# A second-layer tile cut in two around a first-layer tile, late results in other PSUM banks, and a load issued ahead of a transposition

## The chip, the core and the metric

The kernel runs on one core of a Trainium2 chip. The core has a matrix engine (TensorE; PE in the profile, with PEld for its weight loads), a vector engine (VectorE, DVE), an activation engine (ScalarE, ACT), a general engine (GpSimd, POOL) and a queue engine (SyncE, SP) that issues nearly all DMA transfers here. The engines run side by side, each through its own list of instructions in order, and wait for each other by semaphores. Matrix results go to PSUM, eight banks of 512 float32 per partition; everything else on the chip lies in SBUF.

The metric is the device time of one execution in microseconds (us). Lower is better.

## The reference

A retention layer (attention with a decay in place of the softmax) on 8 batches and 8 heads of 576 positions, and behind it a feed-forward block on the 4608 rows that come out:

```python
def _attn_ref(q, k, v):                       # q, k, v: (8, 8, 576, 64)
    scores = scale * np.matmul(q, k.transpose(0, 1, 3, 2))
    gamma = 1.0 - 2.0 ** (-5.0 - np.arange(H, dtype=np.float32))
    rel = pos[:, None] - pos[None, :]
    Dmat = np.where(rel >= 0, gamma[:, None, None] ** rel[None, :, :], 0.0)
    return np.matmul(scores * Dmat[None], v)
...
def _moe_ref(x, w_in, w_out, g_ln):           # x: (4608, 512)
    h = x @ w_in                              # (512, 1024): the first layer
    e = np.exp(h - np.max(h, axis=-1, keepdims=True))
    solu = h * (e / (np.sum(e, axis=-1, keepdims=True) + 1e-09))
    mu = np.mean(solu, axis=-1, keepdims=True)
    var = np.mean((solu - mu) ** 2, axis=-1, keepdims=True)
    ln = (solu - mu) / np.sqrt(var + 1e-06) * g_ln
    return ln @ w_out                         # (1024, 512): the second layer
```

## The kernel before

**Tiles.** The work is cut twice into 36 pieces. A retention step i (0 to 35) takes four heads over a window of 256 positions; a window is two steps, and the last window of every four batches holds the 64 left-over positions of each of them, loaded in four DMAs of 32 partitions per tensor. A feed-forward tile t (0 to 35) takes 128 of the 4608 rows. Tile t needs both steps of its window, so the two kinds of work run interleaved, the tiles some steps behind.

**Names.** One step or tile is a chain of operations, and the code, the diff and the text below call each by its kind and number:

- ldq, ldk, ldv: the loads of a step, on SP's queue (`load`). sq, sk, cv: scaling and casts of them, mostly on POOL.
- T: transposition of q and k on TensorE (`qk_tp`), Te: its evacuation to SBUF on ScalarE. S: scores, 16 matmuls into the bank pair s; mask: VectorE applies the decay. K, st, sm, sc: the running state. I and V: the two parts of the retention result in xy; xe: its evacuation on ScalarE into xT, the first layer's input.
- M1: the first layer of a tile, eight matmuls into h, two banks with one buffer for all tiles (`mm1`). ex: the exponential, on ScalarE. so: h times the exponential, on VectorE, into solu, which has six buffers. When ex and so have read h, the next M1 may write it.
- lx: transposition of solu by a DMA on SP's queue (`ln_dma`). Only the last tile is transposed on TensorE instead (L35, evacuated by Le35).
- va, or bnA and bnB: the variance, on ScalarE or in two halves on VectorE. fx, fin, rs: the scale per row, from the variance of both tiles of a window.
- M2: the second layer of a tile, eight matmuls into one bank (`mm2`). oe: ScalarE scales the result by rs and evacuates it to o_sb, which has three buffers (`o_ev`). out: its store (`store`). The last tile's second layer is done in two halves of columns, M2_35 and M3, with the evacuations oe35 and oz.
- cnt, cs, ci: a test on the row sums at the end, by which a branch picks a general path; it is not taken here.

**Order.** Nothing is scheduled at run time. `ORDER` lists, for each engine, all operations in the order in which the engine runs them; `plan` states each operation's dependencies and the buffers that it takes and frees; `order_ops` merges the five lists into one program order. So a moved word in `ORDER` is a moved instruction on that engine and nothing else, as long as the dependencies allow it.

**Banks of the second layer.** `home(t)` says in which bank M2 of tile t accumulates. Early tiles use s, which they share with the scores: S of a step waits until oe of the M2 before it has read s. Late tiles use o2, two banks taken in turn, which only open when the tile tl of the step transpositions is closed (`bank`), that is when the last Te has run. `OT` is the first tile in o2:

```python
def home(t):
    return "h" if t == NT - 1 else "o2" if t >= OT else "xy" if late(t) and t % 2 else "s"
```

L35 takes a turn in o2 as well.

Of the kernel before, what the change touches and what calls it, by code (L numbers as in the profile page):

```python
# [1081 lines left out]
```

## Time and profile before

| | us |
|---|---|
| median of three runs | 210.21 |
| the three runs | 209.46, 210.21, 211.24 |
| the profiled execution, whole | 208.5 |
| its span, first to last instruction | 206.7 |
| M1 matmuls (L713), 288 of them: busy, mean of one | 68.4, 0.380 |
| M2 matmuls (L786), 296 of them: busy, mean of one | 67.6, 0.373 |
| exponential (L721), mean of one | 1.022 |
| solu (L736 or, with an accumulated sum, L731), mean of one | 1.224 or 1.221 |
| evacuation of xy (L702), mean of one | 0.736 |
| half of a variance on VectorE (L742), mean of one | 0.681 |

The table's durations of matmuls overlap: they are pipelined, so the distance between the starts of two groups says what one costs, not the sum of its durations. A row of the timeline gives the start, the duration, the engine, the source line, the operation with the tile written and the tiles read, how many instructions it merges and, in brackets, how long the engine was idle before it and what released it. All times in the rows count from the start of the span.

### The profile page before, as it was taken

The page shows a single profiled execution, that of the slowest core. Times are in us where ns is not written, and L with a number is a line of the kernel's source. Part 1 is how long each engine was busy: PE and PEld are TensorE (multiplying, and loading weights), DVE is VectorE, ACT ScalarE, POOL GpSimd, SP SyncE. Part 2 cuts the span into 40 slices and gives each one's busy share as a digit, 9 for nine tenths or more (in the row PEclk, how much of TensorE's full clock was granted, in tenths as well). Part 3 has the DMA queues.
Part 4 walks back from the last instruction along what each step waited for, and adds up shares of the span by engine and source line. Part 5 has one row for each costly group of instructions (what it writes and reads, how often), then busy time and mean ns, then how long its engine had stood idle before and what let it go on. Part 6 is the DMA issues. An engine that isn't in the chain of part 4 may idle for free. (4 is left out here: it accounts for less than half of the span.)

```text
span 206.7 us, 8546 instructions
## 1 busy us (share of the span) xinstructions
PE 195.5 (95%) x3576; PEld 108.3 (52%) x3576; DVE 151.4 (73%) x269; ACT 140.7 (68%) x250; POOL 140.2 (68%) x235
## 2 busy tenths in 40 slices
PE   7996989999999999999999999999999999999981
PEld 2442654665665555555555555565555555544450
DVE  6575779995988878688897857896878685725850
ACT  2375798897776667667866687696868756576451
POOL 7434758999997797987678888789795853121110
PEclk9999999999999999999999999999999999999999
DMA  6999999999977869999999999999989557998734
GB/s 175 344 358 331 327 318 292 294 263 290 244 220 222 248 197 306 228 284 219 265 291 174 221 296 239 217 255 227 326 132 280 124 117 201 165 236 212 115 149 103
DMA packets 91112, 49.12 MB, mean 238 GB/s; under 512 B 29624, under 2 KB 84928, under 8 KB 91072
## 3 DMA queue, kind: packets, MB, share of 16 engines
q1 hardware_dynamic: 90832, 48.38, 96.3%
q8 instruction: 28, 0.46, 1.0%
q10 hardware_dynamic: 240, 0.18, 0.4%
q14 instruction: 12, 0.10, 0.2%
HBM read 32.56 MB, written 9.44 MB: 203 GB/s over the span
## 5 line engine op out<-in xcount | busy, mean ns | idle before, releaser
L713 PE MATMUL h_ps<-w_in,xT 128*128 128x512 f16 x288 | 68.4, 380 | 0.2 <-DVE solu L736 0.2
L786 PE MATMUL o_ps<-w2c,ev 128*128 128x512 f16 (+1 forms) x296 | 67.6, 373 | 0.0
L721 ACT ACTIVATE e_sb<-h_ps 128x1024 f32<-128x1024 f32 x36 | 36.8, 1022 | 23.7 <-PE h_ps L713 17.3
L656 DVE TENSOR_TENSOR ret<-s_ps,masks 128x1024 f16<-128x1024 f32 x36 | 43.9, 1219 | 11.2 <-PE s_ps L620 10.7
L786 PEld LDWEIGHTS <-ev 128*128 128x128 f16 x296 | 28.9, 98 | 33.0
L713 PEld LDWEIGHTS <-xT 128*128 128x128 f16 x288 | 25.4, 98 | 29.3 <-ACT xT L702 0.7
L477 POOL TENSOR_TENSOR q<-rawq,small 128x512 f16<-128x512 f32 x34 | 35.3, 1042 | 7.3 <-DMA rawq<-in_q_dram 6.6
L736 DVE TENSOR_TENSOR solu<-h_ps,e_sb 128x1024 f16<-128x1024 f32 x22 | 26.9, 1224 | 18.0 <-ACT e_sb L721 17.8
L477 POOL TENSOR_TENSOR k<-rawk,small 128x512 f16<-128x512 f32 x34 | 35.3, 1042 | 6.3 <-DMA rawk<-in_k_dram 5.9
L795 ACT ACTIVATE o_sb<-o_ps,rs 128x512 f32<-128x512 f32 (+1 forms) x37 | 25.0, 675 | 19.3 <-PE o_ps L786 7.7
L742 DVE BATCH_NORM_STATS2 bs<-solu 128x6 f32<-128x512 f16 x44 | 29.8, 681 | 0.1
L702 ACT CAST xT<-xy 128x512 f16<-128x512 f32 x36 | 26.5, 736 | 2.8 <-PE xy L580 2.7
L697 POOL CAST sbd<-gg 64x256 f16<-64x256 f32 x64 | 25.4, 397 | 2.5
L482 POOL CAST v<-rawv 128x512 f16<-128x512 f32 x28 | 17.0, 610 | 9.9 <-DMA rawv<-in_v_dram 3.9
L731 DVE SCALAR_TENSOR_TENSOR solu<-h_ps,e_sb 128x1024 f16<-128x1024 f32 x14 | 17.1, 1221 | 5.7 <-ACT e_sb L721 5.6
L550 ACT COPY ev<-tl 128x512 f32<-128x512 f32 (+1 forms) x26 | 17.8, 684 | 2.0 <-PE tl L519 1.8
L688 POOL TENSOR_TENSOR gg<-gt,small 128x128 f32<-128x128 f32 x32 | 13.1, 408 | 7.9 <-DVE gt L683 7.5
L776 POOL TENSOR_TENSOR rs<-w,small 128x2 f32<-128x2 f32 x18 | 12.4, 690 | 8.5 <-DVE w L765 7.5
L750 ACT ACTIVATE junk<-solu,su 128x1024 bf16<-128x1024 f16 x14 | 16.1, 1150 | 0.0
L620 PE MATMUL s_ps<-ev 64*64 64x128 f16 x576 | 15.1, 220 | 0.4 <-ACT o_sb L795 0.2
L580 PE MATMUL xy<-ret,v 64*64 64x128 f16 x576 | 14.9, 220 | 0.0
L580 PEld LDWEIGHTS <-sbd 128*128 128x128 f16 x128 | 9.4, 98 | 9.4 <-issue 1.1
(73 smaller groups left out, 204.6 us busy)
## 6 DMA issues: line engine op xcount, KB each, us to landing
rawq<-in_q_dram SPq DMA_DIRECT2D x32, 256.0 KB, 5.0
rawk<-in_k_dram SPq DMA_DIRECT2D x32, 256.0 KB, 5.5
rawv<-in_v_dram SPq DMA_DIRECT2D x32, 256.0 KB, 5.1
out_dram<-o_sb SPq DMA_DIRECT2D x32, 256.0 KB, 3.6
wst<-in_moe_w_in_dram SPq DMA_DIRECT2D x4, 512.0 KB, 6.9
wst<-in_moe_w_out_dram SPq DMA_DIRECT2D x4, 512.0 KB, 7.4
rawk<-in_k_dram SPq DMA_DIRECT2D x16, 64.0 KB, 3.4
rawv<-in_v_dram SPq DMA_DIRECT2D x16, 64.0 KB, 3.5
```

Source lines behind the costliest of these rows:

```text
L477: eng.tensor_tensor(out=t.rearrange("p j h d -> p h j d"), in0=st[i]["r" + nm], in1=g, op=ALU.mult)
L550: nc.scalar.copy(out=t[:, lo:hi].rearrange("p x (r w) -> p r x w", r=2), in_=tls[n].rearrange("p r x w -> p (r x w)").bitcast(FP).rearrang ...
L580: nc.tensor.matmul(start=(c, e) not in begun, stop=False, skip_group_check=True, **kw)
L656: nc.vector.tensor_tensor(out=d["ret"].rearrange("p e h j q -> p (e h) (j q)")[:, :, 0:n], in0=d["s"].rearrange("p e h j q -> p (e h) (j q ...
L697: nc.gpsimd.tensor_copy(out=t[ee[e], :, :, ee[e]], in_=st[i]["gg"][ee[e]])
L702: nc.scalar.copy(out=xT[:, 2 * w : 2 * w + 2, 2 * hf : 2 * hf + 2].rearrange("p c h (q j) -> p c h j q", j=2), in_=xys[i][:, :, 0:256].rea ...
L713: nc.tensor.matmul(out=h_ps[:, hh], lhsT=xT[:, t, dc], rhs=w_in16[:, dc, hh], start=(dc == 0), stop=(dc == 3),)
L721: nc.scalar.activation(out=d["e"], in_=d["h"], func=ACT.Exp, accum_out=se[:, t : t + 1])
L736: nc.vector.tensor_tensor(out=d["solu"], in0=d["h"], in1=d["e"], op=ALU.mult)
L742: nc.vector.bn_stats(out=d["bs"][:, half], in_=d["solu"][:, half * 512 : half * 512 + 512])
L786: nc.tensor.matmul(out=o, lhsT=d["ev"][:, d["lo"] + c], rhs=w2c16[:, c, mm], start=(c == 0), stop=(c == 7))
L795: nc.scalar.activation(out=d["osb"][:, mm], in_=d["o", half], func=ACT.Copy, scale=ws[t // 2]["rs"][:, t % 2 : t % 2 + 1])
```

## The change

Five things are changed, all in the last fifth of the program; no instruction is added to the arithmetic or taken from it.

1. `CUT = 30`: M2 of tile 30 is issued as two groups of four matmuls into the same bank. The first four keep the name M2_30, the last four are the new operation N. M1_34 stands between them, and M2_32 moves behind M1_35.
2. `OT` goes from 30 to 27, and `home` puts tiles 31 and 34 into s. In o2 are now tiles 27, 28, 29, 30, 32, 33 and L35; before, 30 to 34 and L35. M2_27 is therefore the operation that has to wait for the last Te.
3. ScalarE: va31 goes ahead of ex32, xe35 ahead of fx15 and ex33, oe29 ahead of ex34, and oe30 behind ex34.
4. VectorE: bnB32 goes ahead of so34. SP: out29 goes ahead of lx34 and out30 behind it.
5. SP: the load ldq35, four DMAs, goes ahead of the transposition lx26.

```diff
-OT = 30
+OT = 27
+CUT = 30
...
-        "M2_27 I34 V34 S35 M1_32 M2_28 I35 V35 M1_33 M2_29 M2_30 M1_34 M2_31 M2_32 M1_35 M2_33 L35 cs M2_34 M2_35 M3"
+        "M2_27 I34 V34 S35 M1_32 M2_28 I35 V35 M1_33 M2_29 M2_30 M1_34 N M2_31 M1_35 M2_32 M2_33 L35 cs M2_34 M2_35 M3"
...
-        "out20 ldk32 ldv32 lx23 ldk34 ldk33 ldq33 lx24 out21 out22 ldv33 ldq34 lx25 ldk35 lx26 ldq35 out23 lx27 out24  "
+        "out20 ldk32 ldv32 lx23 ldk34 ldk33 ldq33 lx24 out21 out22 ldv33 ldq34 lx25 ldk35 ldq35 lx26 out23 lx27 out24  "
...
-    return "h" if t == NT - 1 else "o2" if t >= OT else "xy" if late(t) and t % 2 else "s"
+    return "h" if t == NT - 1 else "s" if t in (NT - 5, NT - 2) else "o2" if t >= OT else "xy" if late(t) and t % 2 else "s"
...
-            op(f"lx{t}", "SP", "lx", [f"so{t}"], (m + 2, 0.1), [("evl", [f"M2_{t}"])], DUR["ltx"])
+            op(f"lx{t}", "SP", "lx", [f"so{t}"], (m + 2, 0.1), [("evl", ["N" if t == CUT else f"M2_{t}"])], DUR["ltx"])
...
+        cut = t == CUT
+        op(f"M2_{t}", "PE", "M2h" if end or cut else "M2", need, (t + LAG, 3.1), [(home(t), [f"oe{t}"])])
+        if cut:
+            op("N", "PE", "M2h", [f"M2_{t}"], (t + LAG, 4.0))
+        op(f"oe{t}", "ACT", "oeh" if end else "oe", ["N" if cut else f"M2_{t}", f"rs{w}"], (t + LAG + 1, 0.1), [("osb", [f"out{t}"])])
...
-        for c in range(8):
+        for c in range(4 if t == CUT else 8):
             nc.tensor.matmul(
                 out=o, lhsT=d["ev"][:, d["lo"] + c], rhs=w2c16[:, c, mm], start=(c == 0), stop=(c == 7)
             )
+
+    def mm2_rest():
+        d = tk[CUT]
+        for c in range(4, 8):
+            nc.tensor.matmul(
+                out=d["o", 0], lhsT=d["ev"][:, d["lo"] + c], rhs=w2c16[:, c], start=False, stop=(c == 7)
+            )
```

In the rows below the line numbers are those of each kernel; L786 of the kernel before is L774 afterwards (L781 in N), L713 is L701, L568 is L556, and so on. On TensorE, before, one matmul of each tile (each has eight, with weight loads between): M2_30, M1_34, M2_31, M2_32, M1_35, M2_33, L35.

```order
L786 MATMUL o_ps_5274<-w2c16_124,ev_5110 128x512
...
L713 MATMUL h_ps_5291<-w_in16_123,xT_128 128x512
...
L786 MATMUL o_ps_5307<-w2c16_124,ev_5188 128x512
...
L786 MATMUL o_ps_5323<-w2c16_124,ev_5239 128x512
...
L713 MATMUL h_ps_5341<-w_in16_123,xT_128 128x512
...
L786 MATMUL o_ps_5361<-w2c16_124,ev_5286 128x512
...
L531 MATMUL o_ps_5386<-ident_120,solu_5374 128x128
```

The same stretch of TensorE in the changed kernel; the first and the third row have four matmuls each and the same PSUM tile.

```order
L774 MATMUL o_ps_5275<-w2c16_124,ev_5110 128x512
...
L701 MATMUL h_ps_5286<-w_in16_123,xT_128 128x512
...
L781 MATMUL o_ps_5275<-w2c16_124,ev_5110 128x512
...
L774 MATMUL o_ps_5311<-w2c16_124,ev_5194 128x512
...
L701 MATMUL h_ps_5331<-w_in16_123,xT_128 128x512
...
L774 MATMUL o_ps_5351<-w2c16_124,ev_5245 128x512
...
L774 MATMUL o_ps_5365<-w2c16_124,ev_5284 128x512
...
L519 MATMUL o_ps_5386<-ident_120,solu_5363 128x128
```

Four matmuls of the second layer moved behind M1_34, and with them one whole tile moved behind M1_35. SP's queue before, from ldk35 to lx28 (x4: the four DMAs of a load of left-over positions):

```order
L467 DMA rawk_4687<-in_k_dram 32x4x128 x4
L568 DMA_TRANSPOSE ev_4741<-solu_4467 128x8x128
L467 DMA rawq_4753<-in_q_dram 32x4x128 x4
L806 DMA out_0_dram<-o_sb_4620 128x512
L568 DMA_TRANSPOSE ev_4866<-solu_4612 128x8x128
L806 DMA out_0_dram<-o_sb_4763 128x512
L467 DMA rawv_4889<-in_v_dram 32x4x128 x4
L568 DMA_TRANSPOSE ev_4986<-solu_4750 128x8x128
```

The same stretch of SP's queue in the changed kernel:

```order
L455 DMA rawk_4687<-in_k_dram 32x4x128 x4
L455 DMA rawq_4741<-in_q_dram 32x4x128 x4
L556 DMA_TRANSPOSE ev_4814<-solu_4467 128x8x128
L801 DMA out_0_dram<-o_sb_4620 128x512
L556 DMA_TRANSPOSE ev_4866<-solu_4612 128x8x128
L801 DMA out_0_dram<-o_sb_4761 128x512
L455 DMA rawv_4889<-in_v_dram 32x4x128 x4
L556 DMA_TRANSPOSE ev_4986<-solu_4753 128x8x128
```

The second and the third row changed places: lx26 now stands behind eight load DMAs instead of four. ScalarE before, from oe27 to ex34: evacuations of second-layer results are L795, of xy L702, exponentials L721, va is L750, fx is L759.

```order
L795 ACTIVATE o_sb_5139<-o_ps_5116,rs_4982 128x512
L702 CAST xT_128<-xy_5130 128x2x2x2x64
L721 ACTIVATE e_sb_5201,se_129<-h_ps_5176 128x1024
L759 ACTIVATE w_5203<-se_129 128x2
L795 ACTIVATE o_sb_5237<-o_ps_5192,rs_5210 128x512
L750 ACTIVATE junk_5250,mv_5015<-solu_5127,su_5128 128x1024
L759 ACTIVATE w_5253<-se_129 128x2
L721 ACTIVATE e_sb_5264,se_129<-h_ps_5241 128x1024
L750 ACTIVATE junk_5266,mv_5015<-solu_5014,su_5016 128x1024
L702 CAST xT_128<-xy_5212 128x2x2x2x64
L795 ACTIVATE o_sb_5304<-o_ps_5274,rs_5302 128x512
L721 ACTIVATE e_sb_5316,se_129<-h_ps_5291 128x1024
```

The same stretch of ScalarE in the changed kernel:

```order
L790 ACTIVATE o_sb_5143<-o_ps_5120,rs_4982 128x512
L690 CAST xT_128<-xy_5134 128x2x2x2x64
L738 ACTIVATE junk_5192,mv_5015<-solu_5131,su_5132 128x1024
L709 ACTIVATE e_sb_5207,se_129<-h_ps_5180 128x1024
L747 ACTIVATE w_5209<-se_129 128x2
L790 ACTIVATE o_sb_5243<-o_ps_5198,rs_5216 128x512
L690 CAST xT_128<-xy_5218 128x2x2x2x64
L747 ACTIVATE w_5257<-se_129 128x2
L709 ACTIVATE e_sb_5269,se_129<-h_ps_5247 128x1024
L738 ACTIVATE junk_5271,mv_5015<-solu_5014,su_5016 128x1024
L790 ACTIVATE o_sb_5280<-o_ps_5260,rs_5216 128x512
L709 ACTIVATE e_sb_5309,se_129<-h_ps_5286 128x1024
```

va31 (the first L738) now stands ahead of ex32, xe35 (the second L690) ahead of ex33, and the evacuation ahead of ex34 is that of tile 29 instead of tile 30.

More of the change, by code (lines that the diff above doesn't have):

```diff
@@ L63 @@
         "V30 K32 T32 S31 M1_28 M2_24 I31 V31 T33 K33 S32 M1_29 M2_25 I32 T34 V32 S33 M1_30 M2_26 I33 V33 T35 S34 M1_31  "
[1 row of a table removed]
[1 row of a table added]
     ),
     ACT=(
[9 rows of a table removed]
+        "cv0 cv1 Te0 Te1 wi2a wi1a xe0 wi0a wi3a xe1 cv2 ex0 Te2 cv3 Te3 wg4 wg0 ex1 xe2 cv4 Le0 xe3 Te4 Le1 wg6 wg2 cv6  ex2 cv5 va1 cv7 ex3 Te5 va2 Te6 xe4 fx1 fx0 Te7 xe5 va0 Te8 ex4 xe6 Le2 va3 oe0 xe7 Le3 Te9 ex5 oe1 TL8 xe8 ex6  oe2 TL9 xe9 ex7 oe3 xe10 TL10 fx2 ex8 oe4 TL11 xe11 ex9 oe5 fx3 xe12 TL12 fx4 ex10 oe6 xe13 TL13 ex11 oe7 xe14  Te16 ex12 oe8 xe15 Te17 fx5 ex13 oe9 Te18 xe16 ex14 fx6 oe10 va14 xe17 ex15 Te19 oe11 fx7 va15 xe18 ex16 Te20  oe12 xe19 Te21 ex17 oe13 fx8 xe20 Te22 ex18 oe14 xe21 Te23 ex19 oe15 Te24 xe22 va19 ex20 oe16 xe23 Te25 va18  ex21 fx9 oe17 fx10 xe24 Te26 ex22 oe18 xe25 Te27 va22 ex23 fx11 oe19 Te28 xe26 ex24 oe20 va23 xe27 ex25 Te29  oe21 fx12 Te30 xe28 ex26 oe22 Te31 xe29 va26 ex27 oe23 Te32 xe30 ex28 fx13 oe24 va27 xe31 Te33 ex29 oe25 xe32  ex30 Te34 oe26 Te35 xe33 ex31 oe27 xe34 va31 ex32 fx14 oe28 xe35 fx15 ex33 va30 oe29 ex34 oe30 fx16 oe31 ex35  oe32 fx17 oe33 Le35 oe34 oe35 oz"
     ),
     DVE=(
[9 rows of a table removed]
+        "gc sq0 sq1 st0 mask0 st1 wi1b mask1 wi2b wi3b wi0b sk2 sk3 st2 so0 st3 wg5 mask2 mask3 so1 st4 wg7 wg1 wg3  mask4 st6 so2 st5 wc4 wc0 wc7 wc1 st7 so3 mask5 wc5 wc2 wc6 mask6 wc3 mask7 fin0 st8 so4 mask8 st9 bnA4 so5  fin1 bnA5 mask9 st10 bnB4 so6 bnB5 mask10 st11 bnA6 so7 bnA7 mask11 st12 bnB7 so8 bnA8 mask12 st13 bnB6 so9  bnB8 mask13 st14 so10 bnA9 mask14 bnB9 st15 so11 bnA10 mask15 so12 bnA11 mask16 bnB11 bnB10 so13 mask17 st18  bnA13 so14 bnA12 mask18 st19 bnB13 so15 mask19 bnB12 st20 fin7 so16 bnA16 mask20 st21 bnB16 so17 mask21 st22  so18 bnA17 mask22 bnB17 st23 so19 mask23 st24 so20 mask24 bnA20 st25 so21 fin9 mask25 st26 bnB20 so22 bnA21  mask26 st27 bnB21 so23 mask27 st28 so24 bnA24 mask28 bnB24 st29 fin11 so25 mask29 bnA25 st30 so26 mask30 st31  bnB25 so27 mask31 st32 so28 mask32 st33 bnA28 so29 fin13 mask33 bnA29 so30 mask34 bnB29 so31 mask35 bnB28 so32  so33 bnA32 fin15 bnA33 bnB32 so34 bnB33 bnA34 bnB34 so35 cnt bnA35 bnB35 ci"
     ),
```

4 lines of the change are left out of this document (1 added, 3 removed), and 20 rows, old and new, of tables (ACT, DVE, SP).

## The prediction

> **What bounds the kernel now.** I read the page first. Its first two parts say that TensorE is the engine to watch and that its clock is granted in full, so a gain must come out of TensorE's idle time.
>
> ```profile
> span 206.7 us, 8546 instructions
> PE 195.5 (95%) x3576; PEld 108.3 (52%) x3576; DVE 151.4 (73%) x269; ACT 140.7 (68%) x250; POOL 140.2 (68%) x235
> PE   7996989999999999999999999999999999999981
> PEclk9999999999999999999999999999999999999999
> ```
>
> The digits fall below 9 at the start, which the diff leaves alone, and in the last two slices. The table of waits over the last 57 us (waiter, then who released it: total, times, longest in us) names all that TensorE loses there:
>
> ```profile
> PE o_ps L531 <- ACT o_sb L795: 0.7, 1, 0.7
> PE tl L519 <- POOL q L477: 0.3, 1, 0.3
> PE s_ps L620 <- ACT o_sb L795: 0.2, 1, 0.2
> PE h_ps L713 <- DVE solu L736: 0.2, 1, 0.2
> ```
>
> Four waits, 1.4 us in all. TensorE's timeline shows where they stand (start, duration, operation; brackets: idle before it and who ended it):
>
> ```profile
> 170.61 1.89 PE L786 MATMUL o_ps<-w2c,ev 128*128 128x512 f16 x8
> ...
> 173.36 0.32 PE L519 MATMUL tl<-ident,q 64*64 64x64 f16 x16 [0.29 <-POOL q L477]
> ...
> 173.67 0.42 PE L620 MATMUL s_ps<-ev 64*64 64x128 f16 x16
> 174.02 1.90 PE L713 MATMUL h_ps<-w_in,xT 128*128 128x512 f16 x8
> ...
> 178.42 0.42 PE L620 MATMUL s_ps<-ev 64*64 64x128 f16 x16 [0.20 <-ACT o_sb L795]
> 178.77 1.90 PE L713 MATMUL h_ps<-w_in,xT 128*128 128x512 f16 x8
> ...
> 183.13 1.89 PE L713 MATMUL h_ps<-w_in,xT 128*128 128x512 f16 x8 [0.15 <-DVE solu L736]
> 184.86 3.62 PE L786 MATMUL o_ps<-w2c,ev 128*128 128x512 f16 x16
> 188.31 1.89 PE L713 MATMUL h_ps<-w_in,xT 128*128 128x512 f16 x8
> 190.04 3.62 PE L786 MATMUL o_ps<-w2c,ev 128*128 128x512 f16 x16
> 193.49 1.89 PE L713 MATMUL h_ps<-w_in,xT 128*128 128x512 f16 x8
> 195.22 1.89 PE L786 MATMUL o_ps<-w2c,ev 128*128 128x512 f16 x8
> 197.85 0.62 PE L531 MATMUL o_ps<-ident,solu 128*128 128x128 f16 x8 [0.74 <-ACT o_sb L795]
> ...
> 198.52 3.65 PE L786 MATMUL o_ps<-w2c,ev 128*128 128x512 f16 x24
> ```
>
> In order these are M2_26, T35, S34, M1_31, S35, M1_32, M1_33, M2_29+M2_30, M1_34, M2_31+M2_32, M1_35, M2_33, L35, and M2_34 to M3. A tile of eight matmuls takes 1.73 us from start to next start (193.49 to 195.22).
>
> M1 has a second clock. All M1 share the tile h, so M1 of a tile waits until exponential and solu of the tile before have read h:
>
> ```profile
> 180.71 1.02 ACT L721 ACTIVATE e_sb<-h_ps 128x1024 f32<-128x1024 f32 x1 [1.70 <-DVE bs L742]
> 185.06 1.02 ACT L721 ACTIVATE e_sb<-h_ps 128x1024 f32<-128x1024 f32 x1 [0.16 <-PE h_ps L713]
> 181.85 1.23 DVE L736 TENSOR_TENSOR solu<-h_ps,e_sb 128x1024 f16<-128x1024 f32 x1 [0.90 <-ACT e_sb L721]
> 191.38 1.22 DVE L736 TENSOR_TENSOR solu<-h_ps,e_sb 128x1024 f16<-128x1024 f32 x1 [2.52 <-ACT e_sb L721]
> 196.56 1.23 DVE L736 TENSOR_TENSOR solu<-h_ps,e_sb 128x1024 f16<-128x1024 f32 x1 [0.92 <-ACT e_sb L721]
> 196.43 0.68 ACT L795 ACTIVATE o_sb<-o_ps,rs 128x512 f32<-128x512 f32 x1
> ```
>
> These are ex32, ex33, so32, so34, so35 and oe32. M1_32 starts at 178.77, ex32 at 180.71, so32 ends at 183.08 and M1_33 starts at 183.13: two M1 cannot start closer than 4.36 us. The last wait is the same chain: so35 ends at 197.79 and L35, which transposes what so35 wrote, starts at 197.85. (The waits name o_sb there, but oe32, which frees L35's bank, is over at 197.11.)
>
> **The change, part by part.**
>
> *The split.* No matmul is added. Between M1_33 and M1_34 stood two M2 tiles (188.31 − 183.13 = 5.18 us); now a tile and a half, 1.73 + 1.73 + 0.86 = 4.32, just under the chain's 4.36, which takes over with a wait of 0.04. Likewise between M1_34 and M1_35: N 0.86, M2_31 and M1_34 itself, again 4.32 against 4.36. Behind M1_35 two M2 tiles now stand before L35, 5.18 us, while so35 is done 4.30 us after M1_35 (197.79 − 193.49), so L35 waits no more. From M1_33 to L35: before 5.18 + 5.18 + 4.36 = 14.72; after 4.36 + 4.36 + 5.18 = 13.90: **0.82 us gained**. No row shows a group interrupted in its bank. Its bounds: zero, because the passage from M2_30 to M1_34 at 188.31 shows no gap, and 0.04, the slack to the chain that would hide it. I take zero.
>
> *The banks.* M2_27 to M2_29 leave the bank s, so S35 no longer waits for oe27: **0.20 us** between M1_31 and M1_32 (4.75 to 4.55, still above 4.36). M2_27 now needs the two o2 banks open, that is Te35 done:
>
> ```profile
> 172.93 0.69 ACT L795 ACTIVATE o_sb<-o_ps,rs 128x512 f32<-128x512 f32 x1 [0.53 <-DMA out_dram<-o_sb]
> 173.87 0.58 ACT L550 COPY ev<-tl 128x512 f32<-128x512 f32 x1 [0.25 <-PE tl L519]
> ```
>
> The second row is Te35, over at 174.45; M2_27 starts 1.73 after M1_31, at 175.75. A margin of 1.3, no cost. The later bank partners are evacuations that end at least 0.8 us before the bank is needed (oe32, the tightest, needs M1_35 + 3.46 + 0.2 + 0.69 = 4.35 against L35 at 5.18).
>
> *ScalarE, VectorE.* va31 ran here:
>
> ```profile
> 183.57 1.14 ACT L750 ACTIVATE junk<-solu,su 128x1024 bf16<-128x1024 f16 x1
> ```
>
> It moves ahead of ex32, into the 1.70 us of idle time shown there, which begins when xe34 ends. With its 0.19 read (1.14 + 0.19 = 1.33) it leaves 0.4, of which 0.2 goes if M1_31 starts 0.4 later and M1_32 0.2 (below). xe35 (0.74 us by the page's group) takes va31's old place ahead of ex33, so ex33 gets no later. bnB32 (0.68 by its group, and a read-out of 0.2) falls into the 2.52 us before so34. out29 ahead of lx34 waits only for oe29, now done ahead of ex34. All free while these gaps stand.
>
> *The load.* Here the change can lose. SP's queue (start, duration of the issue), then the times from issue to landing of lx26 alone and of the 14 transpositions since 138 us, their issue durations, and who used the load:
>
> ```profile
> 162.62 3.41 SPq L467 DMA_DIRECT2D rawk<-in_k_dram  x4
> 166.12 1.23 SPq L568 DMA_TRANSPOSE ev<-solu  x1
> 167.45 1.96 SPq L467 DMA_DIRECT2D rawq<-in_q_dram  x4
> 169.51 1.32 SPq L806 DMA_DIRECT2D out_dram<-o_sb  x1
> ...
> DMA to landing us min/median/max: 3.1/3.1/3.1
> ...
> DMA to landing us min/median/max: 3.1/3.7/4.4
> L568 SPq DMA_TRANSPOSE ev<-solu x14: 1231/1276/3293, 138.6 to 192.6; - x14
> ...
> 172.26 1.04 POOL L477 TENSOR_TENSOR q<-rawq,small 128x512 f16<-128x512 f32 x1 [0.91 <-DMA rawq<-in_q_dram]
> ```
>
> Order: ldk35, lx26, ldq35 (four issues), out23. With ldq35 ahead, it starts at 166.12 instead of 167.45, sq35 finds its data 1.3 us sooner, and T35's 0.29 us goes. But lx26 is issued 2.03 later (1.96 plus a gap), at 168.15. Today it lands at 166.12 + 3.1 = 169.2 and M2_26, which reads it, starts at 170.61, 1.4 us of cover. Afterwards it lands at 171.25 (3.1), 171.85 (3.7) or 172.55 (4.4), and M2_26 waits s = 0.7, 1.3 or 2.0 us. I take 3.1, its own time, measured behind four such loads too (ldk35). Queued behind M2_26 on TensorE are I33, V33, T35, S34 and M1_31, all later by s − 0.29. out23 keeps its place behind both, hence its time, hence oe26 (172.93, waiting for a store to land). That last row bounds the gain too: S34 (173.67) needs oe26, done at 173.62, so without any s T35's 0.29 would turn into a wait of S34.
>
> *Sum*, M2_26 to L35: before 27.24. After 3.41 − 0.29 + s, then 4.55, 3 × 4.36 and 5.18: 25.93 + s. The gain is 1.31 − s, at most 1.02 because of S34. With s = 0.7 it is **0.6 us**. Behind L35 nothing changes:
>
> ```profile
> 202.26 0.47 ACT L795 ACTIVATE o_sb<-o_ps,rs 128x256 f32<-128x256 f32 x1 [0.41 <-PEq L1037]
> ```
>
> From here to the end of the span are 4.5 us of last evacuation and store. The span goes from 206.7 to 206.1, the profiled execution from 208.5 to 207.9. That execution is below all three runs shown (209.46 to 211.24), so I put the gain on their median: 210.21 − 0.6 = 209.6.
>
> **The rivals.**
>
> *A. The transposition lands in time.* For: the rest of its cover, and T35's wait goes anyway. Against: 1.4 us of cover against 2.03 of delay, and no row under 3.1. Gain 1.02: 209.2.
>
> *B. lx26 is late by far more, and the kernel gets slower.* Place: M2_26. It decides from s = 1.31 on, a landing 3.75 us after issue or an issue held back by 0.65. For: half of the transpositions landed in 3.7 or more, up to 4.4 (s = 2.0, 0.7 lost: 210.9), and an issue took up to 3.29 (2.06 more than here: s = 2.8, 1.5 lost: 211.7). Against: lx26 itself and its 3.1. The Trainium skill's page "DMA: Bandwidth & Descriptors", section "Queues, rings and completion order", says that each DMA engine consumes the descriptors of one issuing queue in ring order, so the transposition cannot pass the four loads put ahead of it; by that rule the price would be the long landing, 0.7 lost instead of 0.6 gained. The trace bears it out only in part: lx26 already stood behind four loads and landed in 3.1.
>
> *C. The chain gets longer.* va31 now stands ahead of ex32. If so31 or xe34 come late, ex32 and M1_33 come late by as much. For: 0.2 us of cover only. Against: so31 does not depend on what moved. About 0.3 to 0.5 lost of the gain: 210.0.
>
> *D. A gain above 1%.* It would need 2.1 us; the waits sum to 1.4. Nothing speaks for it but the spread of the runs, 1.8 us over three.
>
> **How the numbers follow.** The forecast (s from 0.3 to 1.3, gain 0 to 1) gets 0.55, A 0.15, B 0.22, C 0.08. The likeliest time is 209.6. A and the forecast's good end reach 209.2, B's middle case 210.9; with half the runs' spread below, I give 208.4 to 210.9 for 8 in 10; the forecast's own range is 209.2 to 210.2. About 1% (2.1 us) is what a measurement of this kernel can tell from no change. No case reaches that by its mechanism, only with noise or B's worst held issue: faster 0.06, same 0.87, slower 0.07.
>
> **What would show it.** In the profile of the changed kernel: L35 without idle time before it, and M1_33, M1_34, M1_35 at 4.36 us from each other, with small waits on solu (split right); S35 without a wait on o_sb (banks right); T35 without a wait on q, and M2_26 with a wait on the transposition's landing, 0.7 us, S34 to M1_31 about 0.4 late (load right). I am wrong if M2_26 starts at 170.6 without a wait, if the M1 stand 5 us apart, if a bank wait on o_sb shows up before M2_32, M2_33 or L35, or if SP's issue of lx26 takes 2 us or more.

## The result and the profile after

| | us |
|---|---|
| the kernel before, median of 15 runs | 209.52 (208.59 to 211.24) |
| the changed kernel, median of 15 runs | 208.07 (206.80 to 210.64) |
| ratio, 95% interval | 0.9931 (0.9905 to 0.9957) |

The change gains 1.45 us, 0.90 to 1.99 by the interval. That is faster beyond doubt, but within 1%. The forecast was 209.6 with a range of 208.4 to 210.9, so the time lies under the range. Of the 1.5 us between forecast and result, 0.69 is the level (the kernel before has a median of 209.52 over 15 runs, where three runs had shown 210.21), and 0.85 is a gain that was sized too small (0.6 for 1.45). The ratio leaves out executions that lie more than 1.5% above the fastest of their kernel; the medians do not.

The profiled execution of the changed kernel is one of its longest, 209.99 us. Its page says little of why:

```profile
span 208.3 us, 8547 instructions
PE 195.3 (94%) x3576; PEld 108.2 (52%) x3576; DVE 152.1 (73%) x269; ACT 140.7 (68%) x250; POOL 140.5 (67%) x235
PE   7997978999999999799999999999999999999981
PEclk9999999999999999999999999999999999999998
```

TensorE is busy as long as before (195.3 against 195.5) and its clock is granted in full (0.995 on average), so the span of 208.3 holds more idle time, not less. Most of what it has more lies in the front of the program, which the diff leaves alone (one digit of the middle is a 7, where before all are 9): M2_26 came at 172.87, before at 170.61. The rest is in the tail, below. A second profile of the same kernel (experiment e1_again, 206.93 us, span 205.2) reaches M2_26 at 170.76, nearly the moment of before, and is the one to set beside it. TensorE's timeline there, the rows that answer to those of the prediction:

```profile
170.76 1.89 PE L774 MATMUL o_ps<-w2c,ev 128*128 128x512 f16 x8
...
173.05 0.29 PE L507 MATMUL tl<-ident,q 64*64 64x64 f16 x16
...
173.48 0.42 PE L608 MATMUL s_ps<-ev 64*64 64x128 f16 x16
173.83 1.90 PE L701 MATMUL h_ps<-w_in,xT 128*128 128x512 f16 x8
...
177.87 0.39 PE L608 MATMUL s_ps<-ev 64*64 64x128 f16 x16
178.20 1.89 PE L701 MATMUL h_ps<-w_in,xT 128*128 128x512 f16 x8
...
182.55 1.89 PE L701 MATMUL h_ps<-w_in,xT 128*128 128x512 f16 x8 [0.15 <-DVE solu L724]
184.28 2.75 PE L774 MATMUL o_ps<-w2c,ev 128*128 128x512 f16 x12
186.90 1.89 PE L701 MATMUL h_ps<-w_in,xT 128*128 128x512 f16 x8
188.63 1.03 PE L781 MATMUL o_ps<-w2c,ev 128*128 128x512 f16 x4
189.49 1.89 PE L774 MATMUL o_ps<-w2c,ev 128*128 128x512 f16 x8
191.25 1.89 PE L701 MATMUL h_ps<-w_in,xT 128*128 128x512 f16 x8
192.97 3.62 PE L774 MATMUL o_ps<-w2c,ev 128*128 128x512 f16 x16
196.43 0.61 PE L519 MATMUL o_ps<-ident,solu 128*128 128x128 f16 x8
...
197.09 3.65 PE L774 MATMUL o_ps<-w2c,ev 128*128 128x512 f16 x24
```

These are M2_26, T35, S34, M1_31, S35, M1_32, M1_33, M2_29 with the first half of M2_30, M1_34, N (L781), M2_31, M1_35, M2_32 with M2_33, L35, and M2_34 to M3. Of the four waits of before, three are gone (M2_26 has none either), and the 0.15 before M1_33 is as it was. Starts to starts give the balance. I cut the end of the program into four stretches: I from M2_26 to M1_31, II from M1_31 to M1_32, III from M1_32 to L35, IV from L35 to the end of the span. All numbers below are differences of such starts.

| us | I | II | III, from M1 to M1 to L35 | IV |
|---|---|---|---|---|
| before, first profile | 3.41 | 4.75 | 19.08 = 4.36 + 5.18 + 5.18 + 4.36 | 8.90 |
| before, profiled again (e5_before_again) | 3.07 | 4.75 | 19.07 | 9.03 |
| changed, first profile | 3.07 | 4.37 | 18.23 = 4.35 + 4.35 + 4.35 + 5.18 | 9.73 |
| changed, e1_again | 3.07 | 4.37 | 18.23 | 8.78 |

III is 0.85 shorter and II 0.38, and both stay so in every later profile of a kernel with the whole of edits 1 to 4 (a half of them alone is told below). I is longer only in the first profile of before and, by 0.1, in e7 below. IV is 0.95 longer in one profile of the changed kernel.

### The profile page after: what moved, and what is told of

Same layout as the page of the kernel before. It is cut to its first block, busy times and chain, and to the rows that moved or that the text cites. A ratio compares the mean times of both kernels' runs of the same rounds, so it can differ in the third digit from the quotient of the medians.

```text
span 208.3 us, 8547 instructions
## 1 busy us (share of the span) xinstructions
PE 195.3 (94%) x3576; PEld 108.2 (52%) x3576; DVE 152.1 (73%) x269; ACT 140.7 (68%) x250; POOL 140.5 (67%) x235
## 5 line engine op out<-in xcount | busy, mean ns | idle before, releaser
L701 PE MATMUL h_ps<-w_in,xT 128*128 128x512 f16 x288 | 68.4, 380 | 0.2 <-DVE solu L724 0.2
L774 PE MATMUL o_ps<-w2c,ev 128*128 128x512 f16 (+1 forms) x292 | 66.9, 373 | 0.6 <-issue 0.6
L709 ACT ACTIVATE e_sb<-h_ps 128x1024 f32<-128x1024 f32 x36 | 36.9, 1024 | 22.5 <-PE h_ps L701 20.6
L774 PEld LDWEIGHTS <-ev 128*128 128x128 f16 x292 | 28.5, 98 | 33.3 <-issue 0.7
L701 PEld LDWEIGHTS <-xT 128*128 128x128 f16 x288 | 25.4, 98 | 29.4 <-ACT xT L690 0.7
L690 ACT CAST xT<-xy 128x512 f16<-128x512 f32 x36 | 26.5, 736 | 2.8 <-PE xy L568 2.7
L738 ACT ACTIVATE junk<-solu,su 128x1024 bf16<-128x1024 f16 x14 | 16.1, 1151 | 0.0
L568 PE MATMUL xy<-ret,v 64*64 64x128 f16 x576 | 14.9, 220 | 0.0
L568 PEld LDWEIGHTS <-sbd 128*128 128x128 f16 x128 | 9.4, 98 | 9.1 <-issue 1.0
```

Source lines behind the costliest of these rows:

```text
L568: nc.tensor.matmul(start=(c, e) not in begun, stop=False, skip_group_check=True, **kw)
L690: nc.scalar.copy(out=xT[:, 2 * w : 2 * w + 2, 2 * hf : 2 * hf + 2].rearrange("p c h (q j) -> p c h j q", j=2), in_=xys[i][:, :, 0:256].rea ...
L701: nc.tensor.matmul(out=h_ps[:, hh], lhsT=xT[:, t, dc], rhs=w_in16[:, dc, hh], start=(dc == 0), stop=(dc == 3),)
L709: nc.scalar.activation(out=d["e"], in_=d["h"], func=ACT.Exp, accum_out=se[:, t : t + 1])
L774: nc.tensor.matmul(out=o, lhsT=d["ev"][:, d["lo"] + c], rhs=w2c16[:, c, mm], start=(c == 0), stop=(c == 7))
```

## The experiments

### The changed kernel again, and the exchange in and out

Four kernels on one chip: the changed kernel unchanged (e1_again), the kernel before with nothing but the exchange on SP (e2_swap_only), the changed kernel without it (e3_no_swap), and the changed kernel with two edits in the tail (e4_both_tail, told further down).

```diff
 # e2_swap_only: the kernel before, ORDER of SP
-... lx25 ldk35 lx26 ldq35 out23 ...
+... lx25 ldk35 ldq35 lx26 out23 ...
 # e3_no_swap: the changed kernel, ORDER of SP
-... lx25 ldk35 ldq35 lx26 out23 ...
+... lx25 ldk35 lx26 ldq35 out23 ...
```

> The changed kernel once more, for a second profile. Theory P (the prediction): M2_26 waits about 0.7 us for lx26, so M2_26 to M1_31 takes about 3.8 us (3.41 before). Theory Q (formed on the first profile of the changed kernel): no wait there, 3.1 us; M1_31 to M1_32 4.37 (4.75 before); M1_32 to L35 18.2 (19.1 before); and L35 to the end of the span 9.7 (8.9 before), because M2_35 starts 0.7 us late. If that last loss belonged to the one execution only, the tail is 8.9 here. Ratio to the kernel before 0.991 to 0.996 in either.

> The kernel before with only ldq35 ahead of lx26. P: M2_26 waits 0.7 us or more for lx26, the kernel is 0.2 to 0.5 us slower than before (ratio 1.001 to 1.0025). Q: no wait at M2_26; T35 no longer waits for q (0.3), but S34 then waits for oe26, so 0 to 0.3 us faster (ratio 0.9985 to 1.000).

> The changed kernel with lx26 back ahead of ldq35. P: M2_26 loses its wait and the kernel is 0.4 us faster than the changed one (ratio to before about 0.991). Q: T35 waits 0.3 us for q again, the kernel is 0 to 0.3 us slower than the changed one (ratio 0.993 to 0.996).

| | median, us | before beside it | ratio, interval |
|---|---|---|---|
| e1_again | 208.13 | 209.26 | 0.9947 (0.9919 to 0.9975) |
| e2_swap_only | 208.67 | 209.26 | 0.9968 (0.9940 to 0.9997) |
| e3_no_swap | 207.92 | 209.26 | 0.9957 (0.9927 to 0.9986) |

Without the exchange the changed kernel is as fast as with it. Stretch I is 3.08 in e2 and 3.06 in e3. So T35's 0.29 us, which the exchange was to remove, is not there without it either: it belonged to the one execution of before that was profiled. The exchange alone has a median 0.59 lower, at the edge of its interval; no stretch shows where that would come from, and it stays open. Three of its 13 executions took 211.2 to 213.2 us (the longest of 35 of the kernel before took 211.35), and its profile (212.13 us) is one of those. There M2_26 waited; the same showed up in a third profile of the changed kernel (e15_changed_third), whose SP queue and TensorE read:

```profile
163.75 1.97 SPq L455 DMA_DIRECT2D rawk<-in_k_dram  x4
165.81 3.09 SPq L455 DMA_DIRECT2D rawq<-in_q_dram  x4
169.00 1.23 SPq L556 DMA_TRANSPOSE ev<-solu  x1
...
173.79 1.90 PE L774 MATMUL o_ps<-w2c,ev 128*128 128x512 f16 x8 [1.53 <-DMA ev<-solu]
```

The rows are ldk35, ldq35 (1.2 us longer than its 1.9, since one of its four issues was held), lx26, and M2_26. The same SP rows of e1_again, where M2_26 started at 170.76 without a wait:

```profile
161.51 1.96 SPq L455 DMA_DIRECT2D rawk<-in_k_dram  x4
163.57 2.83 SPq L455 DMA_DIRECT2D rawq<-in_q_dram  x4
166.50 1.23 SPq L556 DMA_TRANSPOSE ev<-solu  x1
```

And those of the changed kernel without the exchange, with the tail edits (e17_tail_no_swap_2; M1_30 at 169.69, M2_26 at 171.43):

```profile
163.25 1.96 SPq L455 DMA_DIRECT2D rawk<-in_k_dram  x4
165.30 2.25 SPq L556 DMA_TRANSPOSE ev<-solu  x1
167.65 1.95 SPq L455 DMA_DIRECT2D rawq<-in_q_dram  x4
```

What counts is the cover: the time from the issue of lx26 to the moment at which M2_26 starts when nothing holds it, 1.74 after M1_30. It is 4.26 in e1_again, 3.09 in e15 (M1_30 at 170.35), 6.13 in e17. Over all profiles, with the position of lx26 as only criterion:

| | profiles | cover, us | M2_26 waits |
|---|---|---|---|
| lx26 behind ldk35 | 7 | 4.49 (before, first profile), 6.13, 6.20, 6.31, 6.54, 6.79, 7.83 | none |
| lx26 behind ldk35 and ldq35 | 12 | 2.95, 3.09, 3.19 | 1.6 to 1.7 |
| | | 3.40, 3.47, 3.71, 4.07, 4.09, 4.21, 4.26, 4.34, 5.87 | none |

The exchange takes about 2.4 us of cover (median 6.31 to 3.89), not far from the 2.03 that the prediction reckoned. But the first profile of before, from which I took the 1.4 us that were left, had the smallest cover of its group by 1.6 us, because the fourth issue of ldk35 was held for 1.88 us in it. In nine of twelve profiles the exchange leaves enough. In three it doesn't, and there the transposition also took long: the trace has 4.5 us from issue to landing in e2_swap_only, 4.7 in e13_le35_last and 4.7 in e15_changed_third, against 3.1 in e10 and e11. Seven profiles with the exchange show no landing. Landings of 3.6 to 4.3 occur without the exchange too (e3 3.6, e5 and e8 4.0, e17 4.1, e7 4.3), but there the issue itself took 1.8 to 2.4. Counted from the end of the issue, the landing came after 1.8 to 1.9 us in all of these, in before, e10 and e11, and after 3.3 to 3.5 in the three that waited (3.3 in e12 below too).

The single DMA packets of the trace show which part of the transfer was late. The tile goes in 1024 packets of 256 bytes, and 32 packets of 4 bytes come with the last of them. In the eight other profiles with the exchange in which the issue took 1.23 us, all 32 have started 2.62 us after the start of the issue. In e2, e13 and e15 it is 30 by then, or by 2.66, and the last two follow at 3.5 to 3.6 (in e2 with 17 of the 1024). A packet of 16 KB on a queue that the profile calls instruction runs just ahead of these two: from 2.67 to 3.55 in e13, 2.68 to 3.56 in e15, 2.26 to 3.15 in e2. That it holds them up is not shown: the trace does not say which DMA engine a packet is on, and in e10, e11 and e18 such a packet starts at 2.4 and delays none of the 32. It is no matter of the exchange alone: in e6, with lx26 behind four loads, the tile's packets take until 4.12 us after the start of the issue instead of 2.6, and with 7.83 us of cover that cost nothing.

### What a late transposition costs

The changed kernel with lx26 put behind a store and the next transposition as well, so that it must come late:

```diff
-... ldk35 ldq35 lx26 out23 lx27 out24 ...
+... ldk35 ldq35 out23 lx27 lx26 out24 ...
```

> The changed kernel with lx26 issued still later, behind out23 and lx27, some 2 us. Theory P on its price: once lx26 lands after M2_26 is due, each us of lateness is a us on the end: M1_30 to M2_26 becomes 1.74 + s with s 1 to 2.5, the stretches behind it stay 3.07, 4.37, 18.2 and 8.8, and the kernel is 1 to 2.5 us slower than the changed one (ratio to before 0.999 to 1.007). Rival: the stretches behind it absorb part of it, or lx26 still lands in time (ratio 0.994).

Median 210.04 (before beside it 208.78), ratio 1.0057 (1.0015 to 1.0099), as theory P had it. TensorE's row for M2_26:

```profile
173.44 1.90 PE L774 MATMUL o_ps<-w2c,ev 128*128 128x512 f16 x8 [1.57 <-DMA ev<-solu]
```

M1_30 started at 169.97, so M2_26 is 3.47 behind it instead of 1.74: 1.73 us late. Stretches I to IV are 3.08, 4.37, 18.23 and 8.78, all unchanged. Each microsecond by which M2_26 is late is a microsecond at the end, and the gains of II and III (1.23 together) no longer outweigh it: this version is slower than before.

### Banks alone and the split alone

The kernel before with each half of the change:

```diff
 # e6_banks_only
-OT = 30
+OT = 27
-    return "h" if t == NT - 1 else "o2" if t >= OT else ...
+    return "h" if t == NT - 1 else "s" if t in (NT - 5, NT - 2) else "o2" if t >= OT else ...
 # e7_split_only: CUT = 30 with its code, and in ORDER
-PE   ... M1_34 M2_31 M2_32 M1_35 M2_33 L35 ...
+PE   ... M1_34 N M2_31 M1_35 M2_32 M2_33 L35 ...
-ACT  ... oe30 ex34 oe29 fx16 ...
+ACT  ... oe29 ex34 oe30 fx16 ...
-SP   ... lx33 out30 out29 lx34 out31 ...
+SP   ... lx33 out29 lx34 out30 out31 ...
```

> The kernel before once more, for a second profile. If T35's wait for q and S34's for oe26 belong to the kernel, M1_30 to M1_31 takes 5.14 us again; if they belonged to that one execution, it takes 4.80, as in the runs of the changed kernel with and without the exchanged load. M1_31 to M1_32 4.75, M1_33 to M1_34 and M1_34 to M1_35 5.18 each in either case.

> The kernel before with only the banks of the second layer changed (OT 27, tiles 31 and 34 in s). Theory Q: M1_31 to M1_32 4.37 instead of 4.75, everything else as before, 0.4 us faster (ratio 0.998). The prediction's term for it was 0.20. Rival: the gain of that stretch needs va31 ahead of ex32, or M2_32, which needs tile 29 evacuated, now waits for oe29 behind ex34; then 0 to 0.2 us (ratio 0.999 to 1.000).

> The kernel before with only the split of M2_30, M2_32 behind M1_35, and the order of oe29, oe30 and their stores that goes with it. Q: M1_32 to L35 18.2 instead of 19.1, M1_31 to M1_32 still 4.75, 0.85 us faster (ratio 0.996). Rival: the exponentials of tiles 34 and 35 come later because va31 and xe35 stay where they were, and part of it is lost to the chain (ratio 0.998).

| | median, us | ratio, interval | I | II | III | IV |
|---|---|---|---|---|---|---|
| e6_banks_only | 208.98 | 0.9986 (0.9954 to 1.0018) | 3.07 | 4.37 | 19.06 | 8.84 |
| e7_split_only | 208.52 | 0.9959 (0.9925 to 0.9993) | 3.16 | 4.75 | 18.31 | 9.05 |

The kernel before beside them had 209.31. The interval of e6 includes 1, so what the banks are worth is read from the stretches alone. There the two halves are apart: the banks make II 0.38 shorter and nothing else, the split makes III 0.77 shorter and leaves II. The 0.08 that III lacks in e7 lie between M1_34 and M1_35 (4.43): xe35 keeps its late place on ScalarE there and ends at 188.09, and M1_34's third weight load, which reads its result, starts at 188.14, so M1_34 takes 0.07 longer (1.96 against 1.89), and ex34 and so34, for which M1_35 waits, come as much later. With xe35 ahead of ex33, as in the changed kernel, III has the whole 0.85. The banks' row, TensorE of e6_banks_only (M1_31, V34, S35, M1_32, M1_33):

```profile
173.65 1.90 PE L713 MATMUL h_ps<-w_in,xT 128*128 128x512 f16 x8
...
177.44 0.42 PE L580 MATMUL xy<-ret,v 64*64 64x128 f16 x16
177.68 0.39 PE L620 MATMUL s_ps<-ev 64*64 64x128 f16 x16
178.02 1.89 PE L713 MATMUL h_ps<-w_in,xT 128*128 128x512 f16 x8
...
182.37 1.89 PE L713 MATMUL h_ps<-w_in,xT 128*128 128x512 f16 x8 [0.15 <-DVE solu L736]
```

From M1_31 to S35 it is 4.03; in the first profile of before it was 178.42 − 174.02 = 4.40. The bracket there said 0.20 of idle time. The start moved by 0.37.

TensorE of e7_split_only (S35, M1_32, M1_33, M1_34, M1_35, L35, M2_34):

```profile
178.59 0.42 PE L624 MATMUL s_ps<-ev 64*64 64x128 f16 x16 [0.20 <-ACT o_sb L806]
178.94 1.90 PE L717 MATMUL h_ps<-w_in,xT 128*128 128x512 f16 x8
...
183.30 1.89 PE L717 MATMUL h_ps<-w_in,xT 128*128 128x512 f16 x8 [0.15 <-DVE solu L740]
...
187.65 1.96 PE L717 MATMUL h_ps<-w_in,xT 128*128 128x512 f16 x8
...
192.08 1.89 PE L717 MATMUL h_ps<-w_in,xT 128*128 128x512 f16 x8
...
197.25 0.61 PE L535 MATMUL o_ps<-ident,solu 128*128 128x128 f16 x8
...
198.19 3.63 PE L790 MATMUL o_ps<-w2c,ev 128*128 128x512 f16 x24 [0.21 <-ACT o_sb L806]
```

S35's bank wait is still there, L35's is gone, and a new one of 0.21 stands before M2_34, whose bank in o2 is freed late: M2_34 starts 0.94 behind L35, where it is 0.66 in e1_again. The changed kernel has tile 34 in s and has no such wait. So the two edits belong together: the split gains in III, and the banks keep M2_34 from starting late.

### The tail

The first profile of the changed kernel lost 0.95 us behind L35, where the prediction says that nothing changes. ScalarE's rows there (oe32, oe33, Le35, oe34, oe35):

```profile
197.15 0.69 ACT L790 ACTIVATE o_sb<-o_ps,rs 128x512 f32<-128x512 f32 x1 [0.75 <-PE o_ps L774]
...
199.73 0.69 ACT L790 ACTIVATE o_sb<-o_ps,rs 128x512 f32<-128x512 f32 x1 [1.80 <-DMA out_dram<-o_sb]
200.31 0.58 ACT L536 COPY ev<-o_ps 128x512 f32<-128x512 f32 x1
201.19 0.69 ACT L790 ACTIVATE o_sb<-o_ps,rs 128x512 f32<-128x512 f32 x1 [0.29 <-PE o_ps L774]
202.81 0.47 ACT L790 ACTIVATE o_sb<-o_ps,rs 128x256 f32<-128x256 f32 x1 [0.94 <-PE o_ps L774]
```

TensorE's weight loads and matmuls of M2_35 in the same execution:

```profile
200.94 0.10 PEld L774 LDWEIGHTS <-ev 128*128 128x128 f16 x1 [0.34 <-ACT ev L536]
201.72 1.59 PEld L774 LDWEIGHTS <-ev 128*128 128x128 f16 x15 [0.68 <-issue]
...
201.69 1.91 PE L774 MATMUL o_ps<-w2c,ev 128*128 128x256 f16 x16 [0.59 <-issue]
```

ScalarE is idle for 1.80 us before oe33, until a store gives back the o_sb buffer that oe33 needs (where its matmul alone holds oe33, as in e16, it is 0.81); Le35 is queued behind it on ScalarE and is done at 200.89; M2_35's first weight load, which reads what Le35 wrote, runs at 200.94. Then 0.75 us pass before the first matmul. Between these two the changed kernel has one more instruction, seen in its order on TensorE:

```order
L774 LDWEIGHTS ev
L972 TENSOR_LOAD count
L774 MATMUL o_ps<-w2c_124,ev 128x256
```

This is TensorE's read of the count for the branch behind cnt, cs and ci. Before, it stood one group later, between the first weight load and the first matmul of M3. No word in `ORDER` moved it: the program places it by a time that the planner works out, and that time shifted with the edits. By the trace's record of it, the read starts 0.04 or 0.05 us behind Le35's end in each of five profiles of the changed kernel and takes 0.72 or 0.73. In e1_again it was over 0.1 us before M2_35 was due, so it cost nothing.

Two edits in the changed kernel, Le35 ahead of oe33 and the read later (e4_both_tail, with the exchange; e8_tail_no_swap, without):

```diff
-ACT  ... oe32 fx17 oe33 Le35 oe34 oe35 oz
+ACT  ... oe32 fx17 Le35 oe33 oe34 oe35 oz
-            if in_range is None and start[o.name] > start["ci"] + 0.5:
+            if in_range is None and start[o.name] > start["ci"] + 1.2:
```

> The changed kernel with two edits behind L35: Le35 ahead of oe33 on ScalarE, and the read of the count for the branch one second-layer half later on TensorE (behind M2_35, as in the kernel before). Q: L35 to the end of the span goes from 9.7 back to 8.9 us, the kernel is 0.8 us faster than the changed one (ratio to before 0.989). P, which had nothing behind L35: no difference from the changed kernel (ratio 0.993).

> The changed kernel with lx26 back ahead of ldq35, Le35 ahead of oe33 and the count read behind M2_35. Q: the stretches of the changed kernel (4.37, 4.35, 4.35, 4.35, 5.18), a tail of 8.8 us in every execution and no wait at M2_26: 1.3 to 1.9 us faster than before (ratio 0.991 to 0.994), the best of all. Rival: the exchange of the load was worth 0.3 us; then slower than the kernel with both tail edits and the exchange (0.9923).

e4: median 207.65, ratio 0.9923 (0.9894 to 0.9952), IV 8.79. e8: 208.40 of 8 runs, ratio 0.9925 (0.9886 to 0.9964), IV 8.80. e8's median lies 0.4% under that of before beside it, where the ratio has 0.75%; with eight runs, little hangs on it. No profile of these shows the loss, but nor do e1, e15, e16 and e18 of the changed kernel as it is. So I tried to force it, by putting out30 behind out32, with the read fixed ahead of M2_35's matmuls, with Le35 in either place, and with the read moved behind:

```diff
 # e9_out30_late: the changed kernel
-SP   ... lx34 out30 out31 out32 out33 ...
+SP   ... lx34 out31 out32 out30 out33 ...
-            if in_range is None and start[o.name] > start["ci"] + 0.5:
+            if in_range is None and o.name == "M2_35":
 # e10_out30_late_le35_first: e9, and
-ACT  ... fx17 oe33 Le35 oe34 oe35 oz
+ACT  ... fx17 Le35 oe33 oe34 oe35 oz
 # e11_out30_late_count_late: e9, with the read behind M2_35
```

> The changed kernel with one more edit: the store out30 behind out31 and out32, so that the o_sb buffer that oe33 needs always comes free late. Theory Q: the late tail seen once in the changed kernel is this chain: out30 lands late, oe33 waits, Le35 stands behind oe33, M2_35 waits for Le35, and the read of the count between M2_35's first weight load and its first matmul adds 0.75 us. L35 to the end of the span 10.5 to 12 us (8.8 in a good execution), Le35 2.9 us or more after L35 starts, the first matmul of M2_35 0.75 us after Le35's end. Rival: oe33 has slack, the tail stays at 8.8 to 9.2, and the late tail had another cause.

> As e9, with Le35 ahead of oe33 on ScalarE. Q: M2_35 does not wait, L35 to the end 8.8 to 9.2 us although oe33 is as late as in e9. Rival: the read of the count alone delays M2_35, 9.6 us.

> As e9, with the read of the count behind M2_35's first weight load moved to M3's. Q: M2_35 still waits for Le35, but starts 0.05 us after it instead of 0.75: L35 to the end 0.7 us shorter than in e9 where oe33 is equally late. Rival: the read costs nothing; as e9.

None of the three lost anything: 207.58, 208.08 and 208.22 us, with IV 8.78, 8.78 and 8.77, where e9 was expected to be late. With the stores in that order oe33 took another of the three o_sb buffers than out30's, and in e9 and e11 it started 0.20 us behind L35, held by its matmul alone. So they don't show what a late oe33 costs. So I made Le35 late directly, behind oe34, with the read ahead of M2_35's matmuls (e13_le35_last) and behind them (e14_le35_last_count_late):

```diff
-ACT  ... fx17 oe33 Le35 oe34 oe35 oz
+ACT  ... fx17 oe33 oe34 Le35 oe35 oz
 # e13: the read as in e9; e14: as in e11
```

> The changed kernel with Le35 behind oe34, so that M2_35 must wait for Le35 in every execution. Theory Q (chain of the late tail, second half): the read of the count stands behind M2_35's first weight load, which waits for Le35, so the read starts only then and M2_35's first matmul comes 0.75 us after Le35's end; L35 to the end of the span 10.9 to 11.2 us. Rival: the read runs ahead as soon as the count is there, the first matmul comes 0.05 us after Le35's end, 10.3 us.

> As e13, with the read of the count behind M3's first weight load instead of M2_35's. Q: M2_35's first matmul 0.05 us after Le35's end, L35 to the end 10.2 to 10.4 us, 0.7 less than in e13. Rival: as e13.

210.93 and 209.25 us, with IV 11.00 and 10.51. The rows of e13: Le35, then the first weight load of M2_35 and the rest, then its matmuls.

```profile
201.34 0.58 ACT L536 COPY ev<-o_ps 128x512 f32<-128x512 f32 x1
...
201.97 0.10 PEld L774 LDWEIGHTS <-ev 128*128 128x128 f16 x1 [1.79 <-ACT ev L536]
202.51 1.59 PEld L774 LDWEIGHTS <-ev 128*128 128x128 f16 x15 [0.44 <-issue]
...
202.48 1.91 PE L774 MATMUL o_ps<-w2c,ev 128*128 128x256 f16 x16 [1.80 <-ACT ev L536]
```

The same of e14:

```profile
200.25 0.58 ACT L536 COPY ev<-o_ps 128x512 f32<-128x512 f32 x1
...
200.88 1.64 PEld L774 LDWEIGHTS <-ev 128*128 128x128 f16 x16 [1.79 <-ACT ev L536]
...
200.88 1.92 PE L774 MATMUL o_ps<-w2c,ev 128*128 128x256 f16 x16 [1.30 <-ACT ev L536]
```

From Le35's end to M2_35's first matmul it is 0.56 with the read between (202.48 − 201.92) and 0.05 without (200.88 − 200.83); IV differs by the same 0.5, less than the 0.7 expected, since the read takes 0.49 in e13 and not 0.73. So the second half of the reading is shown: where Le35 is late, the read costs half a microsecond on top. (In the first profile it was 0.75: M2_35 was due 1.74 behind M2_34, at 200.94, and the read had begun only then. In e13 M2_26 also waited 1.6 us, as in e2 and e15.)

The first half is that oe33 waits for a store that the change moved: out30, now behind lx34, is issued 3.9 us ahead of L35 instead of 8.1. Other profiles with this order show the same wait, only shorter. The row of oe33 in e3_no_swap:

```profile
198.30 0.69 ACT L790 ACTIVATE o_sb<-o_ps,rs 128x512 f32<-128x512 f32 x1 [1.10 <-DMA out_dram<-o_sb]
```

oe33 starts 0.20 behind L35 where its matmul alone holds it, 0.32 to 0.49 where it waits for the store (e1, e3, e12, e14, e15), and 1.19 in the first profile of the changed kernel. In e3 it is 0.49, and that already makes M2_35 0.07 late (1.81 behind M2_34 instead of 1.74). So the chain stands in the changed kernel; what made the store land another 0.7 us later in the one profile stays open, and so do the 0.2 us of the 0.95 that M2_35's start doesn't explain.

### More profiles of the changed kernel, and the best version

> The changed kernel, one more profile, to see how often M2_26 waits for lx26 and the tail is late. The stretches that the change decides: 4.37, 4.35, 4.35, 4.35, 5.18. M2_26 without a wait and a tail of 8.8 in most executions (Q); M2_26 with 0.7 us (P).

> The changed kernel, a fourth profile: as for the third, M2_26 without a wait and a tail of 8.8 us (Q), or M2_26 with a wait of 0.7 us for lx26 (P).

> The kernel of e8 again, on the same chip as e18. Theory Q: no execution with a wait of M2_26 (1.6 us, in 3 of 11 profiles of kernels with the exchanged load) and none with a late tail: median 0.2 to 0.5 us under the changed kernel's, and fewer executions 1.5 us or more above the fastest. Profile: M1_30 to M1_31 4.80, then 4.37, 4.35, 4.35, 4.35, 5.18, tail 8.8. Rival: the exchange gains as often as it loses; same median and spread.

> The changed kernel on the same chip as e17. Q: its executions fall into two groups, one near 207.5 us and, for a fifth to a third of them, one 1.5 to 2 us above (M2_26 waits for lx26); median 0.2 to 0.5 us above e17's. Rival: as e17.

e15, e16 and e18 are the changed kernel as it is; e17 is e8 again. One execution each took 209.97 (e15, with M2_26's wait) and 207.96 (e16, without); their stretches I to IV are the same, 3.07, 4.37, 18.23 and 8.78. Timed on one chip, e17 has 207.61 (206.98 to 209.60), ratio 0.9914 (0.9880 to 0.9947), and e18 207.84 (206.91 to 210.62), ratio 0.9915 (0.9883 to 0.9948); the kernel before beside them had 209.63. The medians don't tell the two apart, and e18's executions don't fall into two groups as expected: one of eleven stands apart, at 210.62. What speaks for leaving the exchange out is the profiles, and weakly the long executions: of 38 timed executions of the changed kernel five took over 209.9 us, of 32 without the exchange none did. But of the 12 of e4, which has the exchange and both tail edits, none did either (the longest took 208.50), so the tail may have a share in them. Both beat the kernel before.

## Why the prediction missed

**The split: right.** Forecast 0.82 for stretch III, with M1_33, M1_34 and M1_35 at 4.36 and L35 5.18 behind M1_35. Measured 0.85: 4.35, 4.35 and 5.18. The group that is interrupted in its bank costs nothing: M1_34 is followed by N after 1.73 us, the distance of any tile.

**The banks: mechanism right, size wrong.** I took the 0.20 of the bracket before S35, and left II at 4.55. It came to 4.37, a gain of 0.38 (e6_banks_only alone). The bracket counts idle time from the modelled end of the matmuls before, and pipelined matmuls start before that end: in e6_banks_only V34 runs from 177.44 to a modelled 177.86, and S35, which nothing holds there, starts at 177.68, 0.18 before that end. The distance between two starts, set against the same distance without the wait, is what a wait costs. With 4.37 the chain over h (4.36) is now the bound of this stretch too, which the prediction had as a floor it would not reach: in e1_again so31 ends at 178.15, 0.05 before M1_32 starts, the same distance as from so32 (182.50) to M1_33.

**The load: the step that failed.** "Today it lands at 166.12 + 3.1 = 169.2 and M2_26, which reads it, starts at 170.61, 1.4 us of cover." The delay of 2.03 was about right (2.4 in the median), but the 1.4 came from one execution in which SP was held, and was the smallest margin of the group: where the trace has both ends, e5 of the same kernel has 6.79 − 4.0 = 2.8, and e3, e7, e8 and e17 have 1.9 to 2.7. So the term s = 0.7 is zero in nine of twelve profiles, which is rival A. In the other three it is 1.6 to 1.7, rival B's case, and the execution gives the whole gain back; there the landing of 3.1, which the prediction took as lx26's own, was 4.5 to 4.7. The likeliest case of the prediction lies between the two and occurred in no profile.

The Trainium skill's page "DMA: Bandwidth & Descriptors", section "Queues, rings and completion order", says that each DMA engine consumes descriptors in ring order and that a semaphore increment lands only after every earlier write from that engine, which lets one expect that the transposition cannot land ahead of the loads put before it. The runs show no price for that: behind eight loads as behind four the landing came 1.8 to 1.9 us after the end of the issue, and where it came after 3.3 to 3.5 two of 32 short packets were late, which the number of loads ahead doesn't explain. Its place in the queue moves the issue by 2.4 us and doesn't settle the landing.

**T35's 0.29 and its bound by oe26: a property of one execution.** Stretch I is 3.06 to 3.16 in every other profile, of the kernel before too. The prediction had the exchange remove a wait that is usually not there.

**"Behind L35 nothing changes": wrong in one profile of five.** On TensorE an instruction moved that is no matmul and has no word in `ORDER`, and on SP a store moved behind a transposition. In the first profile IV was 0.95 us longer, 0.75 of it the late start of M2_35; in the others IV is 8.78. That is 0.05 to 0.25 under the profiles with the tail of before (8.83 in e2, 8.84 in e6, 8.90, 9.03), but M2_35 starts 2.40 behind L35 against 2.41, so it is not TensorE's; I did not follow it up.

**The sum.** Lasting gains are 0.38 + 0.85 = 1.2 us on TensorE, and perhaps 0.1 in IV, against 1.45 (0.90 to 1.99) measured; the forecast had 0.20 + 0.82 + 0.29 − 0.7 = 0.6. Two terms of opposite sign that both came from one unusual execution took 0.4 off, the bracket another 0.2. The rest of the miss is the level: I tied the forecast to the median of three runs, though the profiled execution lay below all three. Either half of the miss alone would have left the time inside the range (209.52 − 0.6 = 208.9; 210.21 − 1.45 = 208.8). The prediction also held about 1% to be what a measurement of this kernel can tell from no change; 15 runs of each gave an interval of 0.26% to either side.

## What to carry to other kernels

Take the cover of a transfer (issue to need) from several executions, or at least look in the one at hand for held issues ahead of it: a margin read from a queue that happened to be held is not the usual one. Size a wait on a pipelined engine by the distance between starts, with the wait and without, and not by the idle time before the row. When a planner places instructions by computed times, compare the whole order of each engine, including register reads and branches, since an instruction that the edit doesn't name can land behind a late operand.

## What was not expected of the hardware

- An issue of a load on SP, 0.43 us as a rule, can take 1.2 to 2.2, and at changing places: in the fourth issue of ldk35 (1.88, before, first profile) or in one of ldq35's four (nine of the twelve profiles with the exchange have one of 1.2 or more there); or lx26 itself is held (2.25 instead of 1.24 in e17).
- lx26 landed 1.8 to 1.9 us after the end of its issue in eight profiles, however long the issue took (1.2 to 2.4). Where it landed 1.4 to 1.7 later (e2, e13, e15), two of the 32 short packets at its end were late by about 1 us, and of the 1024 data packets none, or 17 in e2.
- The read of one number by TensorE, placed between a weight load that waits and its matmul, ran only after that weight load was released and delayed the matmul by 0.5 us (e13 against e14).
- The unchanged front varies more than the change gains: without its own wait, M2_26 would start between 170.58 (e6) and 173.06 us (e2). Single spans of two kernels can't be compared at this size; stretches between fixed points agree to 0.01 or 0.02 where no wait differs.
